# Weights of the first expert loaded piece by piece during attention, and a routing turn moved within the expert tiles

## The chip, the cores and the metric

The kernel runs on one core of a Trainium2 chip. The metric is the device time of one execution in microseconds (us). Matrix products run on TensorE (PE in the rows, PEld for its weight loads), most elementwise work on VectorE (DVE) and ScalarE (ACT), copies and scatters on GpSimd (POOL), and nearly all loads and stores are issued by SyncE (SP).

## The reference

Attention with a learned bias on relative positions, then a layer of eight experts of which each token uses one. The softmax scale and the setup of the bias are left out here:

```python
scores = scale * q @ k.T + bias            # 8 batches, 8 heads, 576 x 576, head size 64
attn = softmax(scores)                     # divided by (sum + 1e-9)
x = (attn @ v).transpose(0, 2, 1, 3).reshape(4608, 512)

logits = x @ w_gate + modality_bias[modality_id]
e_idx = argmax(logits, axis=1)             # one of E = 8 experts
gate_w = softmax(logits)[e_idx]            # divided by (sum + 1e-9)
for e in range(E):
    mask = e_idx == e
    h = relu(x[mask] @ w1[e])              # w1[e]: 512 x 1024, 2 MB
    out[mask] = gate_w[mask, None] * (h @ w2[e])   # w2[e]: 1024 x 512, 2 MB
```

## The kernel before

**Attention.** Two heads make a pair; there are 32 pairs, numbered 0 to 31, four to a batch. A pair is worked off in five units (0 to 4), one for each block of 128 (the last: 64) query rows. In this text (30,3) is unit 3 of pair 30. `ORDER` writes out by hand what a unit does: `S` the scores, `e` and `f` the exponentials of the two heads, `C` POOL's copy of the last 64 columns of both heads into a remainder tile `rem` (`compact`), `t` and `T` transposes of earlier exponentials, `R` the transposes of the four remainder tiles (`rtrans`, L474; only after the pair's last unit), `a A b c` the products with v, `x` the store of the result, `L` and `V` loads for later pairs, and `X` and `B` one step each of the routing of the batch before. PE runs about a unit ahead of the others.

**Routing.** `route_steps` holds two lists of steps: `X` takes the next of logits, transposes, `s_rank` (a matmul over one-hots that gives every token its place with its expert), and the rows; `B` takes the next of the small VectorE steps (`s_top`, `s_onehot`, `s_gate`, `s_pos`). A step is skipped for this turn while the other list is not far enough. The rows of a batch go in five blocks: SP loads a block from `xd` (`s_load`, L860), POOL scales it and scatters it into the table `xg` by expert (`s_send`, L866 to L870). The two buffers for blocks alternate, so a load waits for an earlier scatter; and one scatter waits for the one before. In attention the routing of batch 6 ends after pair 31; that of batch 7, the last, runs beside the expert tiles.

**Expert tiles.** An expert works on 256 tokens at a time. The first five tiles are already certain after six batches; `first_table` computes which expert and which rows they have (six steps of small VectorE operations, then a table that SP reads into registers). `first_tiles` hangs these steps, the loads of the first expert's two matrices (`load_w`, into `wst[0]` and `wst[1]`, which lie in the bias memory of pairs that are done), the load of tile 0's rows (`load_rows`, from `xg`) and its preparation (`xprep`, `wsplit_cols`) at units of pairs 28 to 32, where pair 32 stands for the units in which only the end of pair 31 is left. `tile` then has two phases: `phase1` in four groups of 24 matmuls of 256 columns (L1212), each followed by the split of a part of the second matrix (`wsplit`) and a call of `beside`, and `phase2` in two halves of 24 matmuls of 512 columns (L1229), each with a call of `beside`. `moe_first` lists in a string what each of these calls takes of the routing of batch 7: six calls a tile, so places 0 to 5 are tile 0, 6 to 11 tile 1, and so on.

**Queues.** Every engine works in its written order; SP too, so a load that must wait holds up all loads behind it.

Of the kernel before, what the change touches and what calls it, by code (L numbers as in the profile page):

```python
# [21 lines left out]
P = 128  # L22
# [7 lines left out]
E = 8  # L30
# [78 lines left out]
class Attn:  # L109
# [992 lines left out]
    def load_w(self, nm, t, k, dst, cond=None):  # L1102
# [13 lines left out]
        else:  # L1116
            for j in range(2):
                self.nc.sync.dma_start(dst[:, :, DM * j : DM * j + DM], src[:, j::2, :], **kw)

    def load_rows(self, t):  # L1120

        nm, k = self.place(t)
        off = self.reg(nm, k, 1, [mybir.EngineType.SP], E * self.n_tab - TS)
        gx, rows = self.gx[t % 2], self.xg[ds(off, TS), :]
        for g in range(NDC):
            self.nc.sync.dma_start(
                gx[32 * g : 32 * g + 32, 0 : NDC * TS].rearrange("r (a x) -> r a x", x=P),
                rows[:, P * g : P * g + P].rearrange("(a r) x -> r a x", r=32),
            )
        self.nc.sync.dma_start(  # L1130
            gx[:, NDC * TS : NDC * TS + 4].rearrange("p (w x) -> p w x", w=2),
            rows[:, DM : DM + 2].rearrange("(w p) x -> p w x", p=P),
        )
# [152 lines left out]
    def first_tiles(self):  # L1286

        nc = self.nc
        n = self.n_pair - NP
        at = {}  # L1290

        def add(pair, u, f):
            at.setdefault((n + pair, u), []).append(f)

        for k, f in enumerate(self.first_table()):
            add(*divmod(4 + k, 5), f)
        add(2, 3, lambda: self.load_w("first", 0, 0, self.wst[0]))
        add(2, 2, lambda: self.load_rows(0))
        add(3, 0, lambda: self.load_w("first", 0, 1, self.wst[1]))
        add(4, 0, lambda: self.xprep(0, self.Eb[:, next(self.e_next)].rearrange("p h s -> p (h s)")[:, 0 : NDC * TS]))  # L1300
        add(4, 3, lambda: self.wsplit_cols(0))
        return at
# [5 lines left out]
    def moe_first(self):  # L1308


        steps = iter("B,X,X,X,,X,BBX,,X,B,B,X,X,X,X,X,BB,BB,B,B,B,B,BB,B".split(","))

        def beside():
            for op in next(steps, ""):
                if f := self.route_next(self.bg, "XB".index(op)):
                    f()

        if self.K > 1:
            self.load_rows(1)
        if self.K:  # L1320
            self.moe_load(1)
        for t in range(self.K):
            self.tile(t, beside)
        self.route_rest()
# [164 lines left out]
```

## Time and profile before

| | |
|---|---|
| median of three runs | 1026.95 us (1026.75 to 1027.85) |
| the profiled execution | 1026.63 us, its span 1024.40 us |
| PE busy | 979.1 us, 96% of the span |
| VectorE, ScalarE, POOL busy | 72%, 65%, 30% |
| mean granted clock of TensorE | 0.992 |
| longest waits of PE from 560 to 640 us | 6.6 us for POOL's remainder copy, 4.4 us for the one-hot |

The span runs from the first to the last instruction of the profiled execution; the rows below are from it. Attention takes roughly the first 587 us, after some 70 us of bias tables, and the expert tiles the rest. Busy time is only the sum of what an engine did; where time can be won or lost is read from the idle time ahead of an instruction, and from which other engine ended it.

### The profile page before, as it was taken

Reading aid. Unit: us, or ns where it says so; the run is one execution under the profiler, and the core shown is the slowest. Engines: PE = TensorE matmul, PEld = TensorE weight load, DVE = VectorE, ACT = ScalarE, POOL = GpSimd, SP = SyncE. Lnnn points to the kernel's source line nnn. Section 1 sums busy time; section 2 is a strip of 40 time slices with the busy share of each in tenths; the row PEclk is TensorE's granted clock in tenths of the full one; section 3 lists DMA queues with packets and bytes.
Section 4 is the critical chain, followed back from the end, with each engine's and each line's share of the span. In section 5 each row is a group of like instructions: output and inputs, shape, how many; then the busy total and the mean of one; then the engine's idle time right before and its main releaser. Section 6 shows DMA issues by size and latency. Waiting matters only on the chain. (4 is left out here: it accounts for less than half of the span.)

```text
span 1024.4 us, 22706 instructions
## 1 busy us (share of the span) xinstructions
PE 979.1 (96%) x8108; PEld 772.5 (75%) x8108; DVE 741.5 (72%) x1510; ACT 664.8 (65%) x1265; POOL 306.0 (30%) x489
## 2 busy tenths in 40 slices
PE   6789999999999999999999798999999999999997
PEld 2357767777677776777767487889999999898896
DVE  7797778787787877878788476796666665555655
ACT  6677777777778777777777464545556555554544
POOL 1602423625426254262542510611111111111111
PEclk9999999999999999999999899999999999999999
DMA  6977754645646456564557622213115822161610
GB/s 144 190 167 134 197 110 98 135 84 135 115 102 132 85 129 114 112 129 85 135 102 158 182 68 67 94 37 88 43 42 126 295 75 63 33 228 40 209 43 24
DMA packets 328347, 116.36 MB, mean 114 GB/s; under 512 B 284175, under 2 KB 305039, under 8 KB 328227
## 3 DMA queue, kind: packets, MB, share of 16 engines
q1 hardware_dynamic: 322210, 95.81, 42.3%
q0 software_dynamic: 5920, 19.03, 5.1%
q8 instruction: 66, 1.08, 0.4%
q14 instruction: 55, 0.44, 0.1%
q10 hardware_dynamic: 96, 0.00, 0.0%
HBM read 144.34 MB, written 33.34 MB: 173 GB/s over the span
## 5 line engine op out<-in xcount | busy, mean ns | idle before, releaser
L431 ACT ACTIVATE Eb<-Eb,mn 128x576 f32<-128x576 f32 x288 | 221.1, 769 | 45.7 <-DVE mn L416 44.3
L416 DVE CUSTOM_DVE_ANT_0 Eb<-sps,NBm 128x576 f32<-128x576 f32 x256 | 183.6, 754 | 66.1 <-PE sps L402 59.5
L402 PE MATMUL sps<-QK 64*128 64x288 f32 (+1 forms) x1728 | 169.8, 308 | 2.7 <-DVE mn L416 2.5
L402 PEld LDWEIGHTS sps<-QK 64*128 64x128 f32 (+1 forms) x1728 | 132.4, 185 | 46.4 <-DVE mn L416 16.3
L1212 PE MATMUL p<-QK,w1hi 128*128 128x256 f32 x1136 | 162.8, 286 | 1.8 <-DVE QK L1196 1.2
L1212 PEld LDWEIGHTS p<-QK,w1hi 128*128 128x128 f32 x1136 | 148.3, 193 | 6.0 <-DVE QK L1196 2.4
L446 PE MATMUL eps<-idf,Eb 128*128 128x128 f32 x1024 | 146.0, 279 | 4.9 <-DVE eT L333 4.4
L500 PE MATMUL xps<-eT,vraw 128*64 128x288 f32 x1024 | 147.2, 413 | 0.0
L446 PEld LDWEIGHTS eps<-idf,Eb 128*128 128x128 f32 x1024 | 111.2, 141 | 36.0 <-issue 17.8
L1238 POOL DMA_INDIRECT out<-mo,idt x36 | 41.0, 1139 | 315.4 <-ACT mo L1237 255.9
L1215 DVE SCALAR_TENSOR_TENSOR hl<-p,hh 128x512 fp32r<-128x512 f32 x72 | 49.7, 690 | 105.0 <-ACT hh L1214 105.0
L1214 ACT ACTIVATE hh<-p 128x512 fp32r<-128x512 f32 x72 | 43.0, 597 | 122.9 <-PE p L1212 120.8
L436 POOL COPY rem<-Eb 128x128 f32<-128x128 f32 x128 | 37.4, 293 | 255.2 <-ACT Eb L431 252.3
L1229 PE MATMUL p<-w2hi,hh 128*128 128x512 f32 x288 | 112.3, 390 | 0.0
L1229 PE MATMUL p<-w2hi,hl 128*128 128x512 f32 x288 | 112.3, 390 | 0.0
L331 ACT ACTIVATE eT<-eps 128x512 f32<-128x512 f32 x160 | 94.8, 592 | 23.3 <-PE eps L446 21.1
L333 DVE COPY eT<-eps 128x512 f32<-128x512 f32 x128 | 87.3, 682 | 30.1 <-PE eps L446 28.8
L1174 DVE TENSOR_TENSOR w2lo<-NBm,w2hi 128x1024 fp32r<-128x1024 f32 x72 | 89.4, 1242 | 15.9 <-ACT w2hi L1173 15.9
L500 PEld LDWEIGHTS xps<-eT,vraw 128*64 128x64 f32 x1024 | 65.4, 137 | 41.3 <-issue 8.6
L1212 PE MATMUL p<-QK,w1lo 128*128 128x256 f32 x568 | 91.8, 284 | 0.0
L1174 DVE TENSOR_TENSOR w1lo<-NBm,w1hi 128x1024 fp32r<-128x1024 f32 x72 | 84.1, 1230 | 0.0
L1212 PEld LDWEIGHTS p<-QK,w1lo 128*128 128x128 f32 x568 | 78.8, 193 | 0.1
(210 smaller groups left out, 1514.5 us busy)
## 6 DMA issues: line engine op xcount, KB each, us to landing
NBm<-moe_w SPq DMA_DIRECT2D x44, 1024.0 KB
NBm<-moe_w SPq DMA_DIRECT2D x80, 512.0 KB
NBr<-xg SPq DMA_DIRECT2D x80, 128.0 KB
kraw<-k SPq DMA_DIRECT2D x128, 72.0 KB
NBm<-xTb SPq DMA_DIRECT2D x32, 288.0 KB
xd<-xt SPq DMA_DIRECT2D x128, 72.0 KB
vraw<-v SPq DMA_DIRECT2D x64, 128.0 KB
xrb<-xd SPq DMA_DIRECT2D x28, 256.0 KB
```

The source lines that it names most:

```text
L331: self.nc.scalar.activation(out, ps, AF.Copy, scale=scale)
L333: self.nc.vector.tensor_copy(out, ps)
L402: nc.tensor.matmul(self.sps[h][:, half, 0:HS], QK[o, q, qs], QK[o, k, HS * half : HS * half + HS], start=i == 0, stop=i == 2, skip_group_c ...
L416: nc.vector.tensor_tensor_reduce(out=e.rearrange("p (t w) -> p t w", t=2), in0=self.sps[h][:, :, 0:HS], in1=nb.rearrange("p (t w) -> p t w ...
L431: self.nc.scalar.activation(e, e, AF.Exp, bias=mn, scale=-1.0, accum_out=sm)
L446: nc.tensor.transpose(ps[:, k, :], e[:, part, P * k : P * k + P], self.idf)
L500: nc.tensor.matmul(ps[o, :], v[:, h, k, :], self.eT[:, h, k, sl], start=half == 1 and k == 0, stop=half == 0 and k == 3, tile_position=(0, ...
L1174: self.nc.vector.tensor_tensor(l, w, h.bitcast(F32), op=ALU.subtract)
L1212: nc.tensor.matmul(ps[:, a, :], w[:, c, fs], x[:, c, :], start=i == 0, stop=i == len(ops) - 1)
L1214: nc.scalar.activation(hh[:, sl, :], ps, AF.Relu)
L1215: nc.vector.scalar_tensor_tensor(hl[:, sl, :], ps, 0.0, hh[:, sl, :].bitcast(F32), op0=ALU.max, op1=ALU.subtract)
L1229: nc.tensor.matmul(ps, h[:, f, sl], m[:, f, :], start=i == 0, stop=i == len(ops) - 1)
```

## The change

The loads of the first expert's weights are cut into eight pieces of 512 KB, four for each matrix, and hung at eight units: (29,1), (29,3), (30,0), (30,2) for the first matrix, and (30,4), (31,1), (31,3), (32,0) for the second. Before, the first went out whole at (30,3), as four transfers, and the second whole at (31,0), as two. The new `load_part` reads the expert's number into a register of SP each time. The table's six steps move from (28,4)..(29,4) to (26,3)..(27,3), eleven units sooner, which is the first unit after the ranking of batch 5. The load of tile 0's rows moves from (30,2) to (30,4). In `moe_first` the `X` of place 6 moves to place 10.

```diff
+    def load_part(self, k, part):
+
+        e = self.reg("first", 0, 0, [mybir.EngineType.SP], E - 1)
+        src = self.io[("moe_w1", "moe_w2")[k]][ds(e, 1), :, :]
+        dst = self.wst[k]
+        if k == 0:
+            rows = src[:, P * part : P * part + P, :].rearrange("o (c p) f -> p (o c) f", p=32)
+            self.nc.sync.dma_start(dst[32 * part : 32 * part + 32, :, :], rows)
+        else:
+            src = src.rearrange("o (c p) f -> p (o c) f", p=P)
+            self.nc.sync.dma_start(
+                dst[:, part, :].rearrange("p (j f) -> p j f", j=2), src[:, 2 * part : 2 * part + 2, :]
+            )
...
         for k, f in enumerate(self.first_table()):
-            add(*divmod(4 + k, 5), f)
-        add(2, 3, lambda: self.load_w("first", 0, 0, self.wst[0]))
-        add(2, 2, lambda: self.load_rows(0))
-        add(3, 0, lambda: self.load_w("first", 0, 1, self.wst[1]))
+            add(*divmod(k - 7, 5), f)
+        for part, to in enumerate(((1, 1), (1, 3), (2, 0), (2, 2))):
+            add(*to, lambda part=part: self.load_part(0, part))
+        add(2, 4, lambda: self.load_rows(0))
+        for part, to in enumerate(((2, 4), (3, 1), (3, 3), (4, 0))):
+            add(*to, lambda part=part: self.load_part(1, part))
...
-        steps = iter("B,X,X,X,,X,BBX,,X,B,B,X,X,X,X,X,BB,BB,B,B,B,B,BB,B".split(","))
+        steps = iter("B,X,X,X,,X,BB,,X,B,BX,X,X,X,X,X,BB,BB,B,B,B,B,BB,B".split(","))
```

Since a skipped step is taken at a later turn, the ranking, which before was taken at place 6, is now taken at the `X` of place 8, and the row loads at place 10 instead of 11; each scatter behind them comes one place sooner.

SP where attention ends, before. `xrb` are the two buffers of row blocks of batch 6, `xd` holds the attention result, `NBm<-moe_w` is a weight load; ISA rows set addresses:

```order
L1111 DMA NBm<-moe_w 32x4x1024
L860 DMA xrb_92<-xd 128x512
L860 DMA xrb_91<-xd 128x512
L524 DMA xd<-xt_73 32x18x32 x4
L369 DMA vraw_7293<-v 128x4x64 x2
L373 DMA vrem_116<-v 64x64 x2
L860 DMA xrb_92<-xd 128x512
L1090 TENSOR_LOAD tab_first
L1118 ISA
L1118 DMA NBm<-moe_w 128x4x512
```

The same place now, from the first piece of the second matrix on:

```order
L1130 DMA NBm<-moe_w 128x2x512
L524 DMA xd<-xt_73 32x18x32 x4
L369 DMA vraw_7306<-v 128x4x64 x2
L373 DMA vrem_116<-v 64x64 x2
L860 DMA xrb_92<-xd 128x512
L1090 TENSOR_LOAD tab_first
L1130 ISA
L1130 DMA NBm<-moe_w 128x2x512
L860 DMA xrb_91<-xd 128x512
L1090 TENSOR_LOAD tab_first
L1130 ISA
L1130 DMA NBm<-moe_w 128x2x512
```

The row loads L860, which stood behind the first matrix and ahead of the second, now stand between pieces of the second; the first matrix lies ahead of this stretch.

PE in expert tile 1, before. `ohb` is the one-hot, `tri` and `ones` the constants of the ranking, `p` the output banks of phase 1:

```order
L1212 MATMUL p_7593<-QK_75,w1hi 128x256 x8
L1212 MATMUL p_7593<-QK_75,w1lo 128x256 x4
L829 LDWEIGHTS tri
L829 MATMUL xps_80<-ohb,tri 128x48
L831 LDWEIGHTS ones
L831 MATMUL xps_80<-ohb,ones 128x40
```

The same rows now; the three banks are taken in turn, so `p_7593` before is group 0 of tile 1, and `p_7612` now (numbered from `p_7612` to `p_7614`) is group 2:

```order
L1226 MATMUL p_7612<-QK_75,w1hi 128x256 x8
L1226 MATMUL p_7612<-QK_75,w1lo 128x256 x4
L829 LDWEIGHTS tri
L829 MATMUL xps_80<-ohb,tri 128x48
L831 LDWEIGHTS ones
L831 MATMUL xps_80<-ohb,ones 128x40
```

The ranking has moved behind 48 more matmuls; the three VectorE operations that take its result moved with it, and those that make `ohb` stayed where they were.

VectorE where the table begins, before, in (28,4): the scores' evictions are L416, the table's first step L1053 to L1055.

```order
L333 COPY eT<-eps_719 128x4x128
L1053 TENSOR_TENSOR cnt<-base,one 1x8
L974 TENSOR_SCALAR off<-cnt 1x8
L976 TENSOR_TENSOR gk<-off,one 1x144
L982 TENSOR_REDUCE pad_694<-gk 1x8
L1055 MEMSET start 1x8
L416 ISA Eb,mn_4_0_6806<-sps_717,NBr 128x576
```

And now, in (26,3), behind the end of batch 5's ranking:

```order
L824 COPY gi<-ids 128x5
L333 COPY eT<-eps_720 128x4x128
L1053 TENSOR_TENSOR cnt<-base,one 1x8
L974 TENSOR_SCALAR off<-cnt 1x8
L976 TENSOR_TENSOR gk<-off,one 1x144
L982 TENSOR_REDUCE pad_694<-gk 1x8
L1055 MEMSET start 1x8
L849 TENSOR_REDUCE pf_6353<-rks_6331 128x5
```

The step has moved to another pair, two pairs ahead, and stands between evictions there as well.

## Rows read from the trace of the kernel before

Times are microseconds from the start of the span. A row of a timeline is: start, duration, engine, line, operation, out<-in, partitions x elements, count, and in brackets the idle time ahead and what ended it.

**Rows 1.** Page, part 4: shares of the span in the chain that ended last, by engine.

```profile
PE 32%; DVE 4%; ACT 1%; issue 1%; DMA 0%; POOL 0%; POOLq 0%; DVEq 0%; ACTq 0%; SPq 0%
```

**Rows 2.** Timeline of PE where attention ends and expert tile 0 begins.

```profile
571.32 0.49 PE L474 MATMUL xps<-idf,rem 128*128 128x128 f32 x3
578.40 0.47 PE L474 MATMUL xps<-idf,rem 128*128 128x128 f32 x1 [6.59 <-POOL rem L436]
...
579.51 1.06 PE L452 MATMUL eps<-idf,Eb 128*128 128x128 f32 x4
580.51 1.23 PE L491 MATMUL xps<-rT,vrem 128*64 128x288 f32 x4
...
582.70 0.28 PE L457 MATMUL eps<-idf,Eb 128*64 128x64 f32 x4
```

**Rows 3.** Timeline of POOL, the same stretch.

```profile
562.64 1.04 POOL L866 TENSOR_TENSOR xrb<-xrb,rec 128x512 f32<-128x512 f32 x1 [7.54 <-DMA xrb<-xd]
...
568.23 1.04 POOL L870 DMA_INDIRECT xg<-xrb,pos  x1 [1.44 <-issue]
...
577.01 1.03 POOL L870 DMA_INDIRECT xg<-xrb,pos  x1 [5.78 <-DMA xg<-xrb,pos]
578.04 0.30 POOL L436 COPY rem<-Eb 128x128 f32<-128x128 f32 x1
...
585.60 1.82 POOL L870 DMA_INDIRECT xg<-xrb,pos  x1 [1.57 <-DMA xg<-xrb,pos]
```

**Rows 4.** Timeline of SP's DMA queue: second weight matrix.

```profile
568.08 0.97 SPq L1118 DMA_DIRECT2D NBm<-moe_w  x2
```

**Rows 5.** Windows: busy per engine, then PEclk, DMA share, GB/s.

```profile
550.00:560.00 10.00, 9.84 (x92) 7.62 (x90) 7.58 (x23) 7.46 (x18) 2.17 (x4) 1.00 0.99 212
...
575.00:581.00 6.00, 2.60 (x11) 2.08 (x13) 1.01 (x2) 0.60 (x1) 2.49 (x4) 0.51 0.56 203
```

**Rows 6.** Timeline of PE, expert tile 1, around the ranking matmul.

```profile
619.57 0.20 PE L829 MATMUL xps<-ohb,tri 128*128 128x48 bf16 x1 [4.39 <-DVE ohb L816]
...
619.75 2.05 PE L1212 MATMUL p<-QK,w1hi 128*128 128x256 f32 x8
...
624.09 1.12 PE L1212 MATMUL p<-QK,w1hi 128*128 128x256 f32 x8
...
625.53 1.12 PE L1212 MATMUL p<-QK,w1hi 128*128 128x256 f32 x8
```

**Rows 7.** Timeline of PE: remainder turns, one group a pair; two neighbouring pairs, twice.

```profile
460.85 0.60 PE L474 MATMUL xps<-idf,rem 128*128 128x128 f32 x4
...
476.89 0.60 PE L474 MATMUL xps<-idf,rem 128*128 128x128 f32 x4
...
524.10 0.60 PE L474 MATMUL xps<-idf,rem 128*128 128x128 f32 x4
...
541.14 0.60 PE L474 MATMUL xps<-idf,rem 128*128 128x128 f32 x4
```

**Rows 8.** Tile of routed rows, 480 to 520 us: its transfers, issue to landing.

```profile
DMA to landing us min/median/max: 2.9/3.3/4.1
```

**Rows 9.** Timeline of ACT where attention ends.

```profile
573.16 0.59 ACT L331 ACTIVATE eT<-eps 128x512 f32<-128x512 f32 x1
...
589.50 1.05 ACT L1181 CAST w1hi<-NBm 128x1024 fp32r<-128x1024 f32 x1 [2.67 <-DMA xd<-xt]
```

**Rows 10.** Timeline of PE, one pair before the end, the group of rows 2.

```profile
559.07 0.71 PE L491 MATMUL xps<-rT,vrem 128*64 128x288 f32 x4
...
560.57 0.28 PE L457 MATMUL eps<-idf,Eb 128*64 128x64 f32 x4
```

**Rows 11.** Timeline of POOL, expert tile 2: first scatter of the last batch.

```profile
646.30 1.77 POOL L870 DMA_INDIRECT xg<-NBm,pos  x1 [0.61 <-POOL NBm L869]
```

**Rows 12.** Chain that ended last, in order of time: start, duration, what.

```profile
661.23 1.17 DVE xt L1194
```

## The prediction

> **What bounds the kernel now.** I read four views, in this order. The share of busy time first: TensorE is busy for nearly the whole span, so only its gaps and its slow stretches can be won back. Then TensorE's own waits: two of them are far longer than the rest. Then the engines' timelines around these two, each wait followed to what released it. Last the chain that ended last: what is listed of it is TensorE for 32% of the span and VectorE for 4% [rows 1], the whole last third, so a microsecond won ahead of that reaches the end.
>
> The first gap stands where attention ends. The last pair turns its four remainder blocks; three turn at 571.32, the fourth at 578.40, after 6.59 us of waiting for POOL's copy [rows 2]. That copy stands on POOL at 578.04, right behind a scatter of routed rows that issued at 577.01 after waiting 5.78 us for the scatter before it, which had issued at 568.23 [rows 3]. So that scatter took some 8.8 us. Next to it SP issued the two 1 MB halves of the second weight matrix, from 568.08 [rows 4]. The chain is late already at its head: its first rows came after 7.54 us of waiting for a load [rows 3] that stands on SP behind the 2 MB of the first matrix; the ten microseconds from 550 ran at a DMA share of 0.99 and 212 GB/s [rows 5]. After the gap the granted clock is 0.51 (1.2 of 2.4 GHz) from 575 to 581 us [rows 5].
>
> The second gap is in expert tile 1: the ranking matmul waits 4.39 us for the one-hot that VectorE has only just been asked for, and the matmuls behind it run slowly for a while [rows 6]. A third, small loss: the pair in which VectorE makes the first table takes 17.04 us from remainder turn to remainder turn (541.14 - 524.10), and the same place one batch earlier 16.04 [rows 7].
>
> **A: the weights in eight pieces.** Nothing is removed but burst: 4 MB are loaded as before, now in 512 KB pieces, each behind its own register load on SP. What moves: first matrix from (30,3) to (29,1)..(30,2); second from (31,0) to (30,4)..(32,0); rows of tile 0 from (30,2) to (30,4), now behind the first two loads of routed rows.
>
> Nothing holds SP between the third and the fourth piece, so they will go out together, near 546 in the old trace's clock. At the 212 GB/s of [rows 5], 1 MB of weights and two 256 KB row loads end near 554, the rows of tile 0 (0.5 MB) near 557. The first scatter must wait for those rows to be read (it writes the table that they come from), so it issues near 557 to 559. The old one issued 1.5 us behind the 562.64 of [rows 3], hence some 5 us of the chain are won. The second scatter comes no sooner than the remainder copies ahead of it in POOL's order, near 564; beside it runs one 512 KB piece. For its time the ends are 3.3 us (the median from issue to landing where no weights are about [rows 8]) and the 8.8 us beside 2 MB; a quarter of the bytes gives 3.3 + 5.5/4 = 4.7 us, which I take. The third scatter then issues at 568.8 and takes POOL 1.03 us, the remainder copy ends near 570.1, and TensorE wants it at about 571.7: 1.6 us to spare. The wait should vanish.
>
> What is late next: the transposes behind it write a bank that ScalarE empties at 573.16 for 0.59 us [rows 9], a time that the POOL wait does not set. So the group that ran from 579.51 starts at 573.8, which wins 5.7 us. At full clock that group needs half of its 1.00 us, then 560.57 - 559.07 = 1.50 us to the next mark where it took 582.70 - 580.51 = 2.19 [rows 2, 10]: 1.2 us more. A is 6.9 us; its ends are 5.0 (copy 2 us late) and 8.2 (all 6.59 and 1.6 of slow clock).
>
> Cover that must hold: the next cast into the expert's weights waits for the last scatter's reading to end. Before, that scatter issued at 585.60 [rows 3] and the cast ran at 589.50 [rows 9], just in time. Now TensorE wants it 6.9 us sooner, by 582.6; the third scatter issues at 568.8, and two more at 4 to 4.7 us behind it end near 582. I take nothing, but it is the tightest cover: each microsecond past 582.6 costs one. Pieces of the first matrix now stand ahead of the last head pair's loads; 512 KB is 2.4 us at 212 GB/s, and those loads are used a pair (15 us) later. The last piece of the second matrix is wanted only in tile 0's fourth group.
>
> **B: the ranking turn four places back.** VectorE's order keeps the one-hot where it is; the ranking matmuls go behind 48 more matmuls, two groups of 2.88 us (twice the 625.53 - 624.09 = 1.44 of [rows 6]). The one-hot was ready at 619.5; without the wait the old place came at 619.57 - 4.39 = 615.2, so the new one comes at 615.2 + 5.8 = 621.0: no wait, 1.5 us to spare. Won are 4.39 us and the slow stretch: 624.09 - 619.75 = 4.34 for two half-groups that need 2.88, so 1.46. B is 5.85 us.
>
> The three VectorE operations behind the ranking move with it; they add nothing. The row loads and scatters follow one turn sooner, and there the change adds a wait: the rows of tile 3, queued on SP, now come after the first of these scatters. It issued at 646.30 [rows 11]; 3.3 us for it and some 4 for the load give 654, and VectorE turns those rows at 661.23 [rows 12]. Behind them on SP stand only weight loads which the table skips and loads for later tiles; POOL's output writes slip by some 5 us, and nobody waits for them. Cost nothing.
>
> **C: the table eleven units sooner.** The same 29 small VectorE operations leave a pair that lost 17.04 - 16.04 = 1.0 us [rows 7] and enter one that is busy with the previous batch's ranking but has gaps. Ends: 0 (the loss moves along) and 1.0 us. I take 0.6, nearer the gaps.
>
> **Sum.** 6.9 + 5.85 + 0.6 = 13.35 us off the profiled execution's 1026.63 is 1013.3; its time is 0.3 below the median shown, so 1013.6 against 1026.95. By the ends it is 1011.9 (15.05) to 1017.5 (9.4, with 4.4 for B and none for C).
>
> **Rivals.** *POOL's wait stays.* If the 8.8 us scatter was not slowed by the weights beside it, pieces do not help and the fourth remainder is late again. For it: the row names only the scatter. Against: with no weights about, no transfer of these rows took over 4.1 us [rows 8]. It gives B and C alone: 1026.95 - 6.45 = 1020.5. The Trainium skill, DMA: Bandwidth & Descriptors, Queues, rings and completion order, says that each DMA engine takes turns between its queues packet by packet; by that rule a scatter on POOL's queue should not have to sit out 2 MB on SP's, and this rival would be right. The 568.23 and 577.01 of [rows 3] speak against it. Chance 0.14.
>
> *The ranking's saving is given back.* VectorE's work of tile 1 is now pressed into 5.8 us less, and tile 2's second half of the input comes late by as much. For it: VectorE's chain into tile 2 ran up to the wire. Against: that chain starts from TensorE's last group, which moves too. It gives A and C: 1026.95 - 7.5 = 1019.5. Chance 0.07.
>
> *Slower.* One mechanism: the chain of five scatters. Each now has a piece of the second matrix beside it, and the cast at 589.50 waits for the last. If each takes the 8.8 us of [rows 3], the last ends at 557.5 + 44 = 601.5, twelve later than now, and B and C give back 6.45: 1032.5. It decides from 7.7 us a scatter on, where the last ends at 596. Chance 0.04.
>
> *It does nothing.* SP is held so that the pieces pile up where the old burst was, and the ranking's wait moves with it: 1026.95. Chance 0.03.
>
> **How the numbers follow.** The forecast, with its partly late copies, has 0.72. A measurement of this kernel tells about 0.2% (2 us) from no change. Faster by more: 0.72 + 0.14 + 0.07 = 0.93; within: 0.03; slower: 0.04. The range takes the forecast's ends and goes a little towards the rivals at 1019.5 and 1020.5: 1011.5 to 1018.5, which leaves out under 0.2.
>
> **What would show it.** TensorE's waits should no longer list the remainder copy nor the one-hot; the granted clock should stay at 1.00 where attention ends and in tile 1; a wait of about 1.3 us for ScalarE should appear behind the remainder turns; the pair with 17.04 us should read about 16.0. I am wrong in A if a scatter at 564 still takes over 6 us, in B if a wait for VectorE shows at the start of tile 2, in C if the pairs around 480 to 500 us get longer than 15.5.

## The result: faster, by four fifths of what was forecast

| | before | after |
|---|---|---|
| median | 1026.85 us (1026.25 to 1027.85, 4 runs) | 1016.28 us (1014.83 to 1016.79, 4 runs) |
| profiled execution: time, span | 1026.63, 1024.40 us | 1016.41, 1014.2 us |

The ratio is 0.9898, 95% interval 0.9884 to 0.9912: 10.6 us less, where 13.35 were forecast. The time lies within the range, 2.7 us above the forecast. One execution of w2_burst (below) took 1566.35 us at a mean granted clock of 0.56; its ratio is that of the other three.

Where the difference sits is read from the starts of TensorE's rows. I cut both profiled executions at the same marks, so that the lengths add up to the span: the second group of remainder turns (near 97 us, far ahead of every edit), the last pair's remainder turns, the first matmul of tiles 0, 1 and 2, and the second half-group of tile 3.

| stretch (us) | before | after | won | forecast |
|---|---|---|---|---|
| start to second remainder group | 97.20 | 97.89 | -0.69 | 0 |
| to the last pair's remainder turns (C) | 474.12 | 474.16 | -0.04 | 0.6 |
| to tile 0 (A) | 16.55 | 9.75 | 6.80 | 6.9 |
| to tile 1 (cover of A) | 23.65 | 24.23 | -0.58 | 0 |
| to tile 2 (B) | 29.24 | 23.31 | 5.93 | 5.85 |
| to tile 3, second half-group (cover of B) | 24.02 | 25.15 | -1.13 | 0 |
| to the end | 359.62 | 359.71 | -0.09 | 0 |
| sum | 1024.40 | 1014.2 | 10.20 | 13.35 |

Both large terms came to 0.1 us of their size. What is missing is C, two covers (work that was to stay hidden behind other work) that I had priced at nothing, and a start that no edit touches.

TensorE's timeline after, where attention ends (these rows answer to [rows 2]), and the ranking in tile 1:

```profile
572.05 0.60 PE L474 MATMUL xps<-idf,rem 128*128 128x128 f32 x4
574.53 0.66 PE L452 MATMUL eps<-idf,Eb 128*128 128x128 f32 x4 [1.07 <-ACT eT L331]
...
581.80 3.13 PE L1226 MATMUL p<-QK,QK 128*128 128x256 f32 x24
585.12 1.22 PE L1226 MATMUL p<-QK,w1hi 128*128 128x256 f32 x8 [0.20 <-ACT w1hi L1195]
...
615.31 0.20 PE L829 MATMUL xps<-ohb,tri 128*128 128x48 bf16 x1
```

All four remainder blocks turn in one row without a wait; the 1.07 us for ScalarE's bank is the new wait that was forecast at 1.3. The row at 585.12 has a wait for the cast of `w1hi` that was not there before (the same matmuls at 590.83 had none). The ranking has no bracket any more (compare [rows 6]).

POOL in the same stretch (columns as in [rows 3]; L870 is a scatter), and the two windows of [rows 5] together with one of tile 1 (the third number from the end is the granted clock):

```profile
557.69 1.03 POOL L870 DMA_INDIRECT xg<-xrb,pos  x1 [0.75 <-POOL xrb L869]
...
565.25 1.04 POOL L870 DMA_INDIRECT xg<-xrb,pos  x1 [0.61 <-POOL xrb L869]
...
569.44 1.03 POOL L870 DMA_INDIRECT xg<-xrb,pos  x1 [1.69 <-DMA xg<-xrb,pos]
570.80 0.28 POOL L436 COPY rem<-Eb 128x128 f32<-128x128 f32 x1 [0.33 <-ACT Eb L431]
...
575.48 1.03 POOL L870 DMA_INDIRECT xg<-xrb,pos  x1 [2.85 <-DMA xg<-xrb,pos]
...
579.95 1.40 POOL L870 DMA_INDIRECT xg<-xrb,pos  x1 [0.72 <-POOL xrb L869]
```

```profile
550.00:560.00 10.00, 9.84 (x92) 7.67 (x90) 7.52 (x24) 8.02 (x20) 4.67 (x8) 1.00 1.05 238
575.00:581.00 6.00, 6.00 (x53) 3.19 (x52) 3.08 (x6) 1.76 (x3) 3.78 (x8) 1.00 0.69 145
612.00:618.00 6.00, 6.00 (x56) 5.96 (x56) 5.22 (x12) 3.19 (x5) 0.00 (x0) 1.00 0.00 0
```

The first scatter of the kernel before, which [rows 3] leave out:

```profile
564.09 1.03 POOL L870 DMA_INDIRECT xg<-xrb,pos  x1 [0.28 <-POOL xrb L869]
```

So the first scatter issues at 557.69 instead of 564.09. The second, which was the slow one (568.23 to 577.01), now runs from 565.25 to 569.44, and the remainder copy behind the third waits only for ScalarE. The granted clock is 1.00, the upper of its two levels, where it was 0.51 at the end of attention [rows 5].

The late loss, on the timeline of all engines in tile 2 and at the start of tile 3 of the changed kernel, in order of time (SPq is SP's queue of DMAs):

```profile
633.17 0.19 POOL L869 COPY NBm<-gi 128x4 f32<-128x4 f32 x1
633.96 1.01 POOL L870 DMA_INDIRECT xg<-NBm,pos  x1 [0.61 <-POOL NBm L869]
...
637.27 1.93 SPq L1140 DMA_DIRECT2D NBr<-xg  x4
...
640.31 1.22 DVE L1188 TENSOR_TENSOR w2lo<-NBm,w2hi 128x1024 fp32r<-128x1024 f32 x1 [0.24 <-ACT w2hi L1187]
...
642.36 1.02 POOL L870 DMA_INDIRECT xg<-NBm,pos  x1 [5.17 <-DMA NBm<-moe_w]
...
643.14 2.42 DVE L1188 TENSOR_TENSOR w2lo<-NBm,w2hi 128x1024 fp32r<-128x1024 f32 x1 [0.25 <-ACT w2hi L1187]
...
643.41 1.05 POOL L866 TENSOR_TENSOR NBm<-NBm,rec 128x512 f32<-128x512 f32 x1
...
644.40 1.20 POOL L869 COPY NBm<-gi 128x4 f32<-128x4 f32 x1
...
645.48 5.46 DVE L1188 TENSOR_TENSOR w1lo<-NBm,w1hi 128x1024 fp32r<-128x1024 f32 x4
...
650.87 1.23 DVE L1208 STREAM_TRANSPOSE xt<-NBr 128x1024 f32<-128x1024 f32 x1
...
652.13 1.05 ACT L1209 CAST QK<-xt 128x1024 fp32r<-128x1024 f32 x1 [4.27 <-DVE xt L1208]
...
653.23 0.74 PE L1226 MATMUL p<-QK,w1hi 128*128 128x256 f32 x4 [0.80 <-ACT QK L1209]
```

The load of tile 3's rows (L1140) now stands behind the first scatter (633.96), since it reads the table which that scatter writes, and goes out at 637.27. The second scatter writes the same table, so it waits for that load: 5.17 us, to 642.36. (The profile names a weight load that SP issued at about the same time.) So POOL's arithmetic for the third scatter starts at 643.41, beside VectorE's fourth `w2lo`, which takes 2.42 us instead of 1.22. That is the last one ahead of the chain to tile 3's input: four `w1lo`, the transposition, ScalarE's cast, and TensorE waits 0.80 us. The rows themselves were there in time: the transposition has no bracket.

VectorE met POOL in the kernel before too, but one `w2lo` sooner: the third took the time of two, and the fourth, the last ahead of the chain, ran undisturbed. VectorE there:

```profile
651.73 2.38 DVE L1174 TENSOR_TENSOR w2lo<-NBm,w2hi 128x1024 fp32r<-128x1024 f32 x1 [0.24 <-ACT w2hi L1173]
...
654.63 1.21 DVE L1174 TENSOR_TENSOR w2lo<-NBm,w2hi 128x1024 fp32r<-128x1024 f32 x1
```

### The profile page after: what moved, and what is told of

Its sections match the earlier page's. It is cut to its first block, busy times and chain, and to the rows that moved or that the text cites. A ratio compares the mean times of both kernels' runs of the same rounds, so it can differ in the third digit from the quotient of the medians.

```text
span 1014.2 us, 22719 instructions
## 1 busy us (share of the span) xinstructions
PE 977.6 (96%) x8108; PEld 770.4 (76%) x8108; DVE 741.6 (73%) x1510; ACT 664.2 (65%) x1265; POOL 302.8 (30%) x489
## 5 line engine op out<-in xcount | busy, mean ns | idle before, releaser
L416 DVE CUSTOM_DVE_ANT_0 Eb<-sps,NBm 128x576 f32<-128x576 f32 x256 | 183.6, 754 | 67.4 <-PE sps L402 59.4
```

What stands on the lines that cost most here:

```text
L416: nc.vector.tensor_tensor_reduce(out=e.rearrange("p (t w) -> p t w", t=2), in0=self.sps[h][:, :, 0:HS], in1=nb.rearrange("p (t w) -> p t w ...
```

## The experiments

The same stretches for all profiled executions. The medians carry the variation of the start (96.1 to 98.0 us here, see the end), so small edits are told by their own stretch.

| | start | C | to tile 0 | tile 0 | tile 1 | tile 2 to 3 | end | median, us |
|---|---|---|---|---|---|---|---|---|
| before | 97.20 | 474.12 | 16.55 | 23.65 | 29.24 | 24.02 | 359.62 | 1026.85 |
| after | 97.89 | 474.16 | 9.75 | 24.23 | 23.31 | 25.15 | 359.71 | 1016.28 |
| turn_alone | 96.99 | 474.11 | 16.58 | 23.50 | 23.28 | 24.98 | 359.46 | 1020.97 |
| pieces_table | 96.06 | 473.78 | 9.75 | 24.52 | 30.27 | 24.05 | 359.87 | 1020.69 |
| rows_old | 96.75 | 473.73 | 9.75 | 25.06 | 23.28 | 24.25 | 359.78 | 1014.70 |
| table_alone | 96.71 | 473.80 | 15.23 | 23.65 | 29.18 | 24.52 | 359.51 | 1026.20 |
| no_w2 | 97.52 | 473.92 | 9.74 | 23.67 | 23.28 | 25.16 | 359.91 | 1013.49 |
| w2_burst | 96.18 | 473.87 | 12.90 | 23.52 | 23.28 | 25.25 | 359.50 | 1016.71 |
| w1_burst | 97.82 | 474.01 | 13.90 | 26.99 | 23.28 | 24.91 | 359.49 | 1020.36 |
| best1 | 97.16 | 474.94 | 9.73 | 23.50 | 23.29 | 24.07 | 359.71 | 1014.36 |
| best2 | 97.97 | 474.16 | 9.75 | 23.49 | 23.28 | 24.14 | 360.01 | 1014.12 |
| best3 | 96.64 | 473.38 | 9.74 | 23.50 | 23.30 | 24.20 | 359.74 | 1012.75 |

The kernel before, run beside them, had medians of 1026.67 (first four), 1027.09 (next four) and 1026.51 (last two).

**The parts one by one.** First the ranking turn alone, on the kernel before:

```diff
-        steps = iter("B,X,X,X,,X,BBX,,X,B,B,X,X,X,X,X,BB,BB,B,B,B,B,BB,B".split(","))
+        steps = iter("B,X,X,X,,X,BB,,X,B,BX,X,X,X,X,X,BB,BB,B,B,B,B,BB,B".split(","))
```

> The kernel before with only the ranking turn moved (the step string of the changed kernel). Theory: the 4.39 us wait for the one-hot and its slow stretch go (5.9 us won by the start of tile 2), but the scatters of the last batch now start ahead of the load of tile 3's rows, POOL's row arithmetic meets VectorE's last w2lo, and tile 3 starts some 1.1 us late: 1026.9 - 4.8 = 1022.1. Rival 1, the loss at tile 3 belongs to the weights in pieces: 1021.0, no ScalarE wait at tile 3. Rival 2, VectorE's pressed work is late at the start of tile 2: a wait there of more than 1 us, 1022 or more.

Measured: 1020.97 us, ratio 0.9949 (0.9935 to 0.9963). The time is that of rival 1, but its interval reaches from 1020.0 to 1022.9 and holds both. The stretches decide: tile 1 takes 23.28 us instead of 29.24, and tile 2 to 3 takes 24.98 instead of 24.02, with the same kind of wait at tile 3:

```profile
658.18 0.74 PE L1212 MATMUL p<-QK,w1hi 128*128 128x256 f32 x4 [0.64 <-ACT QK L1195]
```

So the loss at tile 3 belongs to the ranking turn, not to the pieces. The wait at the start of tile 2 is 0.25 us, as before (0.26): the pressed work of VectorE is not late there.

Then the rest without the ranking turn, that is the changed kernel with the old step string:

```diff
-        steps = iter("B,X,X,X,,X,BB,,X,B,BX,X,X,X,X,X,BB,BB,B,B,B,B,BB,B".split(","))
+        steps = iter("B,X,X,X,,X,BBX,,X,B,B,X,X,X,X,X,BB,BB,B,B,B,B,BB,B".split(","))
```

> The changed kernel with the old step string: weights in pieces and the table moved, ranking turn where it was. Theory: 6.8 us won at the remainder turns, 0.6 given back at the first cast of the expert's weights, 0.2 from the table: 1026.9 - 6.4 = 1020.5, and the one-hot wait of 4.4 us is there again. Rival, the parts help each other (the ranking wait shrinks or grows with the earlier start): more than 1 us away from 1020.5.

Measured: 1020.69 us, ratio 0.9950 (0.9936 to 0.9964), the time that the theory gave. In its trace the stretch to tile 0 is 9.75 us, as in the changed kernel, but tile 1 takes 30.27 instead of the 29.24 of before, although the wait for the one-hot is as long as in [rows 6]. The slow stretch behind it lasts longer:

```profile
612.15 0.20 PE L829 MATMUL xps<-ohb,tri 128*128 128x48 bf16 x1 [4.38 <-DVE ohb L816]
...
612.33 2.05 PE L1226 MATMUL p<-QK,w1hi 128*128 128x256 f32 x8
...
615.04 1.91 PE L1226 MATMUL p<-QK,w1hi 128*128 128x256 f32 x8
...
617.60 1.24 PE L1226 MATMUL p<-QK,w1hi 128*128 128x256 f32 x8
```

In [rows 6] the matmuls were back at 1.12 us at 624.09, some 4.5 us behind the ranking; here only the fourth such row is, at 619.15. One wait, two prices. table_alone, which has the old loads, takes 29.18 there; this is one trace against two, and whether the pieces or chance made the difference is not shown.

**Why tile 3 starts late.** The ranking stays at its new place, and the row loads and scatters behind it go back to theirs:

```diff
-        steps = iter("B,X,X,X,,X,BB,,X,B,BX,X,X,X,X,X,BB,BB,B,B,B,B,BB,B".split(","))
+        steps = iter("B,X,X,X,,X,BB,,X,B,B,X,X,X,X,X,BB,BB,B,B,B,B,BB,B".split(","))
```

> The changed kernel with the ranking turn at its new place, but row loads and scatters of the last batch at their old place (the first scatter again behind the load of tile 3's rows). Theory: the 0.8 us wait for ScalarE at the start of tile 3 goes, since POOL's arithmetic falls where it fell before: 1016.3 - 1.1 = 1015.2. Rival, the loss comes from VectorE having 5.9 us less for the same work: the wait stays, 1016.3.

Measured: 1014.70 us, ratio 0.9886 (0.9871 to 0.9901). Tile 2 to 3 takes 24.25 us instead of 25.15, and the wait for ScalarE is gone. VectorE's four `w2lo` and POOL beside them, on the timeline of this kernel:

```profile
633.78 1.45 DVE L1188 TENSOR_TENSOR w2lo<-NBm,w2hi 128x1024 fp32r<-128x1024 f32 x1 [0.24 <-ACT w2hi L1187]
...
636.66 2.41 DVE L1188 TENSOR_TENSOR w2lo<-NBm,w2hi 128x1024 fp32r<-128x1024 f32 x1 [0.24 <-ACT w2hi L1187]
...
636.91 1.06 POOL L866 TENSOR_TENSOR NBm<-NBm,rec 128x512 f32<-128x512 f32 x1
...
639.59 1.21 DVE L1188 TENSOR_TENSOR w2lo<-NBm,w2hi 128x1024 fp32r<-128x1024 f32 x1
...
639.77 1.93 POOL L870 DMA_INDIRECT xg<-NBm,pos  x1 [0.66 <-POOL NBm L869]
...
642.36 1.51 DVE L1188 TENSOR_TENSOR w2lo<-NBm,w2hi 128x1024 fp32r<-128x1024 f32 x1 [0.25 <-ACT w2hi L1187]
```

The second scatter waits 0.66 us, not 5.17, and VectorE is slowed at the second `w2lo`, where there is time behind it to catch up, and only a little at the fourth: 1.51 us instead of 2.42, 0.91 less, while the stretch is 0.90 shorter. VectorE has the same work in the same time as in the changed kernel, so the rival falls: what cost 1.13 us was where the collision fell. The total does not show this. The profiled span is 1.6 us shorter, but 1.14 of it lie in the start and 0.43 in C, which this edit does not touch, and tile 0 happened to take 0.83 us more: TensorE waited 1.00 us for the cast of `w1hi` in it, 0.20 in the changed kernel.

**The table alone.** The kernel before with one line changed:

```diff
-            add(*divmod(4 + k, 5), f)
+            add(*divmod(k - 7, 5), f)
```

> The kernel before with only the first table moved eleven units sooner. Theory after the result: the pair from 476.89 grows by 0.8 us to 16.35 and the pair from 524.10 shrinks by 1.0 to 16.03, so 0.2 us is won: 1026.7. Rival, the prediction's 0.6 us: 1026.3, with pairs around 480 to 500 us no longer than 15.5.

Measured: 1026.20 us, ratio 0.9997 (0.9987 to 1.0006); the times do not tell 0.2 from 0.6 us. TensorE's remainder turns do (each row is one pair behind the one before):

```profile
476.25 0.60 PE L474 MATMUL xps<-idf,rem 128*128 128x128 f32 x4
492.60 0.60 PE L474 MATMUL xps<-idf,rem 128*128 128x128 f32 x4
...
524.32 0.60 PE L474 MATMUL xps<-idf,rem 128*128 128x128 f32 x4
540.33 0.60 PE L474 MATMUL xps<-idf,rem 128*128 128x128 f32 x4
```

In the kernel before these two pairs took 15.51 us (from 476.89 of [rows 7] to the row here) and 17.04:

```profile
492.40 0.60 PE L474 MATMUL xps<-idf,rem 128*128 128x128 f32 x4
```

With 16.35 and 16.01 one pair pays 0.84 us and the other gets back 1.03. The loss moved along, all but 0.2 us. (The stretch to tile 0 is 1.3 us shorter here; the edit does not touch it. The wait behind the slow scatter was 6.59, 6.21 and 5.4 us in three executions that all have the old loads.)

**Which burst slowed the scatters.** Each burst put back alone, and the second matrix left out:

```diff
-        for part, to in enumerate(((2, 4), (3, 1), (3, 3), (4, 0))):
-            add(*to, lambda part=part: self.load_part(1, part))
+        add(3, 0, lambda: self.load_w("first", 0, 1, self.wst[1]))
```

> The changed kernel with the first matrix in pieces, but the second again as two halves of 1 MB at its old place. Theory: the chain's head is as early as in the changed kernel (first scatter 557 to 558), but the second scatter, at about 565, has 2 MB beside it and takes 8 to 9 us; the fourth remainder turn waits some 3 us for POOL's copy: about 1019. Rival, queues share by turns and the scatter does not sit the weights out: second scatter under 5 us, 1016.3.

```diff
-        for part, to in enumerate(((1, 1), (1, 3), (2, 0), (2, 2))):
-            add(*to, lambda part=part: self.load_part(0, part))
+        add(2, 3, lambda: self.load_w("first", 0, 0, self.wst[0]))
```

> The changed kernel with the second matrix in pieces, but the first again as two halves of 1 MB at its old place. Theory: POOL waits some 7 us for the first routed rows again, all five scatters come about 5 us later, the fourth remainder turn waits 2 to 3 us for POOL and the cast of w1hi comes late too: 1018.5 to 1020. Rival, only the second matrix's burst did harm: 1016.3.

```diff
-        for part, to in enumerate(((2, 4), (3, 1), (3, 3), (4, 0))):
-            add(*to, lambda part=part: self.load_part(1, part))
```

> The changed kernel without the four loads of the first expert's second weight matrix (left out altogether: the first expert computes with other data there). It tells whether the scatters are slow because of weights beside them. Theory: the third scatter of the batch, which takes 6.0 us in the changed kernel (569.44 to 575.4), takes no more than 4.3; the last scatter ends over 1 us sooner; TensorE does not wait for the cast of w1hi, and 0.6 us are won: 1015.7. Rival, the scatter's length is its own, or that of the row loads beside it: it stays at 6 us and the time at 1016.3.

Measured: w2_burst 1016.71 us (ratio 0.9897, 0.9878 to 0.9917), w1_burst 1020.36 (0.9932, 0.9915 to 0.9948), no_w2 1013.49 (0.9868, 0.9852 to 0.9885). POOL with the second matrix in a burst, then without the matrix:

```profile
563.25 1.04 POOL L870 DMA_INDIRECT xg<-xrb,pos  x1 [0.61 <-POOL xrb L869]
...
571.57 1.03 POOL L870 DMA_INDIRECT xg<-xrb,pos  x1 [5.81 <-DMA xg<-xrb,pos]
```

```profile
568.95 1.03 POOL L870 DMA_INDIRECT xg<-xrb,pos  x1 [1.79 <-DMA xg<-xrb,pos]
...
573.32 1.03 POOL L870 DMA_INDIRECT xg<-xrb,pos  x1 [1.27 <-DMA xg<-xrb,pos]
```

Beside 2 MB a scatter takes 8.3 us from issue to issue, without weights 4.4; the 6.0 us of the changed kernel's third scatter (569.44 to 575.48) lie between, with one 512 KB piece (SP, 569.55) and a 256 KB row load (568.70) beside it. The row load is not what slows it: without the matrix it goes out as close ahead of that scatter (568.20), and the scatter takes 4.4 us. In the kernel before, too, the two scatters behind the burst took only 4.1 and 4.5 us (577.01, 581.12, 585.60). Weights are not all, though: the fourth scatter of no_w2 takes 5.8 us (573.32 to 579.10), with no weights about but SP's stores of attention's rows. So the theory of slow scatters holds, and the theory of what follows holds in the trace: TensorE waits 2.93 us for the remainder copy in w2_burst, and its stretch to tile 0 is 12.90 us, 3.15 more than in the changed kernel. But its time is within 0.5 us of the changed kernel, where 1019 was expected: its tile 0 gets back 0.7 and its profiled execution began 1.7 us faster, and its few other runs, of which no trace is kept, do not tell whether they did too. By the time alone I could not say that the second burst matters; by the stretches it costs 2.4 us.

In w1_burst the head is late again: POOL waits 3.88 us for its first rows and 2.91 for the rows of tile 0 to be read, the turn waits 3.96, and the cast of `w1hi` comes 1.74 us late (expected were some 7 us for the rows and 2 to 3 for the turn). With tile 0 it is 0.7 us worse there than before any change (40.89 against 40.20 us from the last remainder turn to tile 1). So the pieces of the second matrix alone win nothing; the pieces of the first do, and beside them those of the second win the 2.4 us above.

Without the second matrix tile 0 takes 23.67 us instead of 24.23, and TensorE does not wait for the cast: 0.56 of the 0.58 us lost there are the price of its late pieces. Two expectations were missed: the last scatter issues only 0.2 us sooner, counted from the remainder turns, where over 1 was expected, since the fourth takes 5.8; and the time is 2.8 us below the changed kernel's, of which the stretches behind the start show 0.6. The rest is not explained.

**Versions that beat both.** best1 takes the scatters back (as rows_old), moves the third and fourth piece of the second matrix to (32,0) and (32,3), behind the fourth scatter, and the table two units later:

```diff
-            add(*divmod(k - 7, 5), f)
+            add(*divmod(k - 5, 5), f)
...
-        for part, to in enumerate(((2, 4), (3, 1), (3, 3), (4, 0))):
+        for part, to in enumerate(((2, 4), (3, 1), (4, 0), (4, 3))):
...
-        steps = iter("B,X,X,X,,X,BB,,X,B,BX,X,X,X,X,X,BB,BB,B,B,B,B,BB,B".split(","))
+        steps = iter("B,X,X,X,,X,BB,,X,B,B,X,X,X,X,X,BB,BB,B,B,B,B,BB,B".split(","))
```

> The changed kernel with three further edits: row loads and scatters of the last batch at their old place; the first table two units later, so that it lies within the one pair that holds no routing; the third and fourth piece of the second matrix later, behind the fourth and fifth scatter. Theory: 1.1 us at tile 3, 0.85 us in the pair around 480 to 494 (15.5 again, and the next pair no longer than 15.5), 0.6 to 1.0 us at the cast of w1hi (third scatter 4.2 us): 1016.3 - 2.8 = 1013.5. Rival, VectorE has no room in the next pair either: that pair grows by 0.8, 1014.4.

best2 is best1 with the table where the change put it (the first of these three edits undone):

> The changed kernel with two further edits: row loads and scatters of the last batch at their old place, third and fourth piece of the second matrix behind the fourth and fifth scatter; the first table where the change put it. Theory from the run before this (best1): tile 3 starts without a wait (1.0 us), the cast of w1hi is not waited for (0.6 to 0.8 us), and the pairs around 480 to 510 us are as in the changed kernel (16.35 and 15.4), which is 1.0 us less than with the table two units later: 1016.3 - 1.7 = 1014.6 on a median, and 1.0 us below best1. Rival, what tile 3 and the cast gain is lost again behind them: 1016.3.

best3 is best2 with the table spread:

```diff
-            add(*divmod(k - 7, 5), f)
+            add(*((-1, 0), (-1, 1), (-1, 2), (-1, 3), (0, 1), (0, 3))[k], f)
```

> best2 with the six steps of the first table at units (27,0), (27,1), (27,2), (27,3), (28,1) and (28,3), so that none stands in the pair with the ranking nor at (27,4) and (28,0), where the table two units later made TensorE wait 1.31 us for VectorE's maximum. Theory: the pair around 477 to 493 takes 15.5 us again (0.85 won), the next stays at 15.4 to 15.6: 1013.7. Rival, the table costs about 0.8 us wherever it stands, since VectorE has no room there: one of the two pairs behind grows by 0.8, and the time is that of best2.

Measured: best1 1014.36 us (0.9879, 0.9863 to 0.9896), best2 1014.12 (0.9876, 0.9857 to 0.9895), best3 1012.75 (0.9863, 0.9843 to 0.9883). In all three tile 0 takes 23.5 us and tile 2 to 3 24.1 to 24.2: the two covers are whole again. best2 was to be 1.0 us below best1; it is 0.2 by the medians and 0.4 from the second remainder group to the end. In best1 the rival was right and more: the pair with the ranking is back at 15.50, but the next takes 17.05 (492.23 to 509.28), with 1.31 us of waiting for VectorE's maximum behind the table's last steps. best3 leaves those units out:

```profile
476.31 0.60 PE L474 MATMUL xps<-idf,rem 128*128 128x128 f32 x4
491.79 0.60 PE L474 MATMUL xps<-idf,rem 128*128 128x128 f32 x4
507.45 0.60 PE L474 MATMUL xps<-idf,rem 128*128 128x128 f32 x4
523.82 0.60 PE L474 MATMUL xps<-idf,rem 128*128 128x128 f32 x4
```

15.48, 15.66 and 16.37 us: there is room for the table, but not in any of the three places with six neighbouring units that were tried. From the second remainder group to the end best3 takes 913.9 us, the changed kernel 916.3, the kernel before 927.2.

## Why the prediction was right, and where it was short

**A, 6.9 us: right, 6.80.** Its steps held: SP sent the third and fourth piece together (545.84), the first scatter issued at 557.69 (forecast 557 to 559; its row names POOL's copy, not the reading of tile 0's rows), the remainder copy did not wait for the chain, and ScalarE's bank became the next wait. One step was off without harm: without weights I took 3.3 us for a scatter [rows 8] and 4.7 beside a piece; the second scatter took 4.2 with a piece sent 1.7 us ahead of it, and 4.3 in no_w2. [Rows 8] are loads, and a scatter is no load.

**The tight cover: mis-sized.** "Two more at 4 to 4.7 us behind it end near 582": the third took 6.0, because SP sends a piece just behind it, and the last issued at 579.95 instead of some 577.5. ScalarE's cast, after:

```profile
584.02 1.05 ACT L1195 CAST w1hi<-NBm 128x1024 fp32r<-128x1024 f32 x1 [3.25 <-DMA xd<-xt]
```

I had said that each microsecond past 582.6 costs one; by that the cast would have cost 1.4 us, and the tile lost 0.58. The mark was too early: TensorE came to these matmuls 2.96 us behind the tile's start in the kernel before (587.87, 590.83), so after 581.80 it needs the cast, 1.05 us long, at 583.7. best1 and no_w2 show that the late pieces are the cause. That the cast waits for the last scatter is argued: the row names a store, in the kernel before [rows 9] as here, but the cast ran 3.9 and 4.1 us behind that scatter's issue.

**B, 5.85 us: right, 5.93.** The one-hot was ready at 614.05, the ranking came at 615.31, with 1.3 us to spare where I gave 1.5, and the clock stayed up.

**"Cost nothing", behind B: the step that failed.** I followed the load of tile 3's rows behind the first scatter, saw that the rows would be there in time, and stopped. They were. But the same order makes the second scatter wait for the load, moves POOL's arithmetic, and POOL beside VectorE doubles a `w2lo`: 1.13 us. I asked who waits for the queue, not what the released work would run beside. The Trainium skill, SBUF — State Buffer, section "Who interferes with whom", says that a VectorE instruction with two SBUF inputs contends with a GpSimd instruction that reads SBUF, and calls the shared ports an exclusive lock. This case's rows agree: `w2lo` takes 2.42 us beside POOL and 1.22 alone, POOL's copy (L869) 1.20 instead of the 0.19 that it takes ahead of the first scatter.

**C, 0.6 us: mis-sized, 0.2.** "Nearer the gaps" was a guess at a pair in which VectorE also makes a ranking. table_alone shows 0.84 us lost and 1.03 won, the changed kernel 0.84 and 1.01. The C stretch of the result shows none of the 0.2 us left, but it varies from 473.73 to 474.16 us over the eight executions with this table. The mark that I set (a pair longer than 15.5) is what showed it.

**The rivals.** POOL's wait did not stay, and the scatter was slowed by the weights (8.3 us beside 2 MB, 4.4 without). The Trainium skill, DMA: Bandwidth & Descriptors, section "Queues, rings and completion order", has queues take turns packet by packet. Beside 2 MB the scatter still took 1.9 times as long here; whether that is what taking turns leaves to it, no run tells. The ranking's saving was not given back at tile 2, as I had it, but a fifth of it at tile 3, by another way. The chain of slow scatters stayed below its 7.7 us each.

**The remainder.** 0.69 us of the shortfall lie ahead of every edit, and 0.09 behind them all.

## What to carry to other kernels

When a step moves, follow not only who waits for it but what it now runs beside: an engine that nobody waits for can still slow one that somebody waits for. A cover that is called tight should be given a price from the slowest row of its kind, not from the middle one. And gains of a microsecond are read between marks in the trace, since the total varies by more than that.

## What the runs showed of the hardware

The start varies. Before the second remainder group, where all twelve programs do the same, the profiled executions took 96.06 to 97.97 us. The windows there show one thing that goes with it: in some executions the granted clock drops where TensorE has been short of inputs (2.53 of 5 us busy). First the changed kernel (97.89), then w2_burst (96.18):

```profile
45.00:50.00 5.00, 2.53 (x21) 1.03 (x17) 2.46 (x6) 2.96 (x5) 0.00 (x0) 0.84 1.04 197
50.00:55.00 5.00, 5.00 (x63) 3.74 (x59) 5.00 (x13) 3.59 (x6) 0.00 (x0) 0.81 0.93 196
...
65.00:70.00 5.00, 5.00 (x49) 3.15 (x44) 4.00 (x9) 3.11 (x6) 0.00 (x0) 0.66 0.43 113
```

```profile
45.00:50.00 5.00, 3.03 (x22) 1.22 (x25) 3.17 (x7) 3.06 (x5) 0.00 (x0) 1.00 1.04 202
50.00:55.00 5.00, 5.00 (x64) 2.22 (x55) 5.00 (x13) 4.14 (x6) 0.00 (x0) 1.00 0.95 197
...
65.00:70.00 5.00, 4.89 (x69) 3.00 (x61) 4.46 (x13) 4.77 (x12) 0.29 (x1) 1.00 0.39 111
```

Executions with two such stretches took 97.5 to 98.0 us, with one 96.1 to 97.2, with none (a single one) 96.2. The clock is not the whole of it, since those with one drop differ by 1.1 us, and nothing was tried. The other thing is the price of a wait in clock: the same 4.4 us for the one-hot was followed by two slow half-groups in two executions and by three in a third, 1.0 us apart. What sets the number was not tried.
